# A batch's units all before its output products, attention steps of one shape side by side, and the last 64 rows of even and odd heads paired

## The chip, the cores and the metric

The kernel runs on one core of one Trainium2 chip. The time is that of one execution on the device, in microseconds (us); the median of three runs is given. TensorE (PE, with its weight loads as PEld), VectorE (DVE), ScalarE (ACT) and SyncE (SP, which issues all DMAs here) each work through their own instructions in order and wait for one another by semaphores.

## The reference: what is computed

Eight batches with eight heads, 576 positions and 64 values per head go through an attention with 32 memory slots per head. Then a bilinear feed-forward layer follows, whose last two products have nothing between them.

```python
a = phi - np.max(phi, axis=2, keepdims=True)
a = np.exp(a)
a = a / (np.sum(a, axis=2, keepdims=True) + 1e-09)      # softmax over the 576 positions
k_m = np.einsum('bhsm,bhsd->bhmd', a, k)                # 32 memories per head
v_m = np.einsum('bhsm,bhsd->bhmd', a, v)
scores = scale * np.matmul(q, k_m.transpose(0, 1, 3, 2))
...                                                     # softmax over the 32 memories
attn_out = np.matmul(attn, v_m)
x = attn_out.transpose(0, 2, 1, 3).reshape(B * S, H * D)
a = x @ w1
b = x @ w2
h = a * b @ w3
return h @ w_out
```

All arrays are float32. `w1` and `w2` are 512 x 1024, `w3` is 1024 x 1024, `w_out` is 1024 x 512.

## The kernel before

**What is computed how.** The kernel forms W = w3 w_out once, so that the feed-forward layer is one product with w1, one with w2, and one with W. It also multiplies w1 and w2 by each batch's v_m, which gives a matrix M per batch (`memory_weights`); so a batch's a and b come directly from its attention probabilities. To keep float32 accuracy at the speed of float32r, the operands of the large products are split into a high and a low part (`split`, lines 107 to 109: a ScalarE cast and a VectorE subtraction), and each product is the sum of three matmuls: high with high, high with low, low with high.

**A batch.** The 576 positions are two halves of 288 (`n`). `ab_unit(b, n, f, g)` makes 128 of the 1024 columns of a and b for one half, six matmuls each (line 407), copies a out of PSUM (line 416), multiplies (line 418) and splits the product into gh and gl (108 and 109). There are 16 such units per batch. `out_part(b, n, o, part, g, v)` does half of the sum for 128 of the 512 outputs, 12 matmuls (line 432); after the second half ScalarE copies the result to `osb` (line 437) and SP stores it (line 439). There are 16 of these too.

**Attention of the next batch.** Between the units and output products of batch b stand the steps of batch b+1, as functions in `attention(b)`: `top` takes the maximum of phi (line 144), `exp` (150), `norm` (155, 156), `turn0` and `turn4` transpose the exponentials on TensorE (165) to bring positions onto partitions, `mem` multiplies them with k and v (176), `blocks` transposes the memories back and lays them out (192 to 196), `sc0` and `sc1` make the scores of one half each (207), which VectorE transposes out of PSUM (216). `se`, `sn` and `pr` are the softmax and the split of the probabilities, one half each. The four quarters of M follow (line 263), each evacuated by one `split`.

**Positions in chunks.** 576 positions are four chunks of 128 and a last one of 64. In `turn4` that last chunk takes two transposes, of the even and of the odd heads (`t` = 0 and 1), and in `mem` it takes matmuls on 64 rows and 32 columns of the array, where the others use 128 rows and 32 columns. The loop runs over `t` outside and over chunks inside, so that the two shapes alternate.

**PSUM.** Eight banks: `ps_ab` has two sets of an a and a b bank, for the units; `ps_o` has two for the output products; `ps_x` is one pair of banks (`psum_pair`), which all attention steps and M share, one after the other.

**Order of the work.** The order on TensorE and SP is that of the program, fixed by hand in the lists `START`, `PLAN0` and `PLAN1`; the order on VectorE and ScalarE is set by a planner that simulates the program. `PLAN1` (batches 1 to 7) numbers 32 slots: eight units of the first half, eight output parts of it, eight units of the second half, eight output parts. After each slot come the steps that the plan names, so `sc0`, `sc1` and the four M stand apart from each other. `PLAN0` is for batch 0, whose 16 units come first.

**The start.** `START` works off the list `tasks`: each "C" (`next_tile`, `convert`) turns one tile of weights, which arrive as 64-bit floats, into float32 with ScalarE and VectorE (lines 339 to 344), and fetches a later one. "W00" and so on are products for W (line 354), "K" splits a finished block of W into Wh and Wl. The attention of batch 0 and two quarters of its M stand among them. The last four tiles are converted among the units of batch 0, from tiles that otherwise hold kv and q; the loads of batch 1's kv, q and phi come behind them in SP's order.

Of the kernel before, what the change touches and what calls it, by code (L numbers as in the profile page):

```python
# [29 lines left out]

PLAN0 = {
# [4 lines left out]
}  # L36


@with_exitstack
def memory_attention__then__bilinear_ffn_kernel(  # L40
# [21 lines left out]
    nc = tc.nc  # L62
# [11 lines left out]
    NBLK = S // M  # L74
    chunks = [(c, min(P, S - c)) for c in range(0, S, P)]
    scale = 1.0 / D**0.5
# [27 lines left out]
    def psum_pair():  # L104
        return ps_x.tile([P, 2, 512], F32, name="x")

    def split(hi, lo, src):
        nc.scalar.copy(out=hi, in_=src)  # L108
        nc.vector.tensor_tensor(out=lo, in0=src, in1=hi.bitcast(F32), op=ALU.subtract)  # L109
# [9 lines left out]
    def load_kv(b):  # L119
        t = []  # L120
        for i in range(0, len(chunks), 2):
            c, n = chunks[i]
            m = min(2, len(chunks) - i)
            x = att.tile([P, m, 8 * 2 * D], F32, name=f"kv{i}", tag=f"kv{i}")
            nc.sync.dma_start(out=x[:n], in_=kv[b, c : c + m * n].rearrange("(c p) h x -> p c (h x)", c=m))
            t += [x[:, j] for j in range(m)]
        loaded["kv", b] = t

    def load_q(b):
        t = att.tile([P, NG, S], F32, name="q", tag="q")  # L130
        nc.sync.dma_start(out=t, in_=qT[b].rearrange("g p s -> p g s"))
        loaded["q", b] = t


    ready = {}

    def attention(b):
# [16 lines left out]
        def norm():  # L154
            nc.vector.tensor_scalar_add(v["sm"], v["sm"], 1e-9)
            nc.vector.reciprocal(out=v["sm"], in_=v["sm"])
            a = att.tile([P, len(chunks) * NT * P], F32, name="a", tag="a")
            v["a"] = a.rearrange("p (c t x) -> p c t x", t=NT, x=P)

        def turn(i):  # L160
            ps = psum_pair().rearrange("p k (c t x) -> p (k c) t x", c=2, t=NT)
            some = chunks[i : i + 4]
            for k, (c, n) in enumerate(some):
                for t in range(NT):
                    nc.tensor.transpose(ps[:n, k, t], v["ph"][:, t, c : c + n], ident)  # L165
            n = some[0][1]
            nc.scalar.copy(out=v["a"][:n, i : i + len(some)], in_=ps[:n, : len(some)])

        def memories():
            kvt = loaded.pop(("kv", b))  # L170
            v["kvm"] = att.tile([P, NT, 2 * D], F32, name="kvm")
            ps = psum_pair()
            for t in range(NT):
                for i, (c, n) in enumerate(chunks):
                    for h in range(4):
                        nc.tensor.matmul(  # L176
                            ps[h * M : (h + 1) * M, t, : 2 * D],
                            lhsT=v["a"][:n, i, t, h * M : (h + 1) * M],
                            rhs=kvt[i][:n, (2 * h + t) * 2 * D : (2 * h + t + 1) * 2 * D],
                            start=i == 0,  # L180
                            stop=i == len(chunks) - 1,
                        )
            for t in range(NT):
# [13 lines left out]

        def scores(n):

            if n == 0:  # L200
                v["q"] = loaded.pop(("q", b))
                s_sb = att.tile([P, len(chunks) * NT * P], F32, name="s_sb", tag="a")
                v["s"] = s_sb[:, : NT * S].rearrange("p (n k m) -> p n k m", n=2, m=M)
            ps = psum_pair()[:, :, :HALF]
            for g in range(NG):
                for t in range(NT):
                    nc.tensor.matmul(  # L207
                        ps[g * M : (g + 1) * M, t],
                        lhsT=km[b % 2][t * D : (t + 1) * D, g],
                        rhs=v["q"][t * D : (t + 1) * D, g, n * HALF : (n + 1) * HALF],  # L210
                        start=True,
                        stop=True,
                    )
            nb = NBLK // 2
            for t in range(NT):
                nc.vector.transpose(
                    out=v["s"][:, n, t * nb : (t + 1) * nb], in_=ps[:, t].rearrange("p (k m) -> p k m", m=M)
                )
# [25 lines left out]

        steps = {"top": top, "exp": exp, "norm": norm, "mem": memories, "blocks": blocks}
        steps |= {f"turn{i}": lambda i=i: turn(i) for i in range(0, len(chunks), 4)}
        for name, f in (("sc", scores), ("se", soft_exp), ("sn", soft_norm), ("pr", probs)):
            steps |= {f"{name}{n}": lambda f=f, n=n: f(n) for n in range(2)}
# [5 lines left out]
    def memory_weights(b):  # L254

        ms = ready["M", b] = []

        def step(q):
            ps = psum_pair()
            for g in range(NG):  # L260
                for t in range(NT):
                    d = slice((1 - t) * D, (2 - t) * D)
                    nc.tensor.matmul(  # L263
                        ps[g * M : (g + 1) * M, t],
                        lhsT=vm[b % 2][d, g],
# [5 lines left out]
            ml = const.tile([P, NT, 2, FQ], F32R, name=f"ml{q}", tag=f"m{m_tags[2 * q + 1]}")  # L271
            src = ps.rearrange("p t (w f) -> p t w f", w=2)
            split(mh, ml, src)
            ms.append((mh, ml))

        return [lambda q=q: step(q) for q in range(NQ)]

# [34 lines left out]
    def convert(i):  # L312
# [13 lines left out]
        elif i % 2:  # L326
            u = att.tile([P, len(chunks) * NT * P], I32, name="ua", tag="a")
        else:
            u = att.tile([P, 2, S], F32R, name="al", tag="al", bufs=2).rearrange("p t s -> p (t s)").bitcast(I32)
# [44 lines left out]
    with tc.tile_pool(name="init", bufs=1) as init:  # L374
# [4 lines left out]
        for what in START:  # L379
# [4 lines left out]
            elif what[0] == "K":  # L384
                keep(int(what[1]), int(what[2]))
            elif what == "M":
                m0.pop(0)()
            elif what in ("phi", "kv", "q"):
                {"phi": load_phi, "kv": load_kv, "q": load_q}[what](0)
            else:  # L390
                steps[what]()
# [48 lines left out]

    def load(what, b):
        if b < B:
            {"phi": load_phi, "kv": load_kv, "q": load_q}[what](b)

    for b in range(B):
        g, v = {}, {}
        ab = [lambda n=n, f=f: ab_unit(b, n, f, g) for n in range(2) for f in range(NF)]
        out = [
            lambda n=n, o=o, part=part: out_part(b, n, o, part, g, v)
            for n in range(2)  # L450
            for o in range(NO)
            for part in range(2)
        ]
        if b == 0:
            next_tile()
            order = [n * NF + 2 * q + f for q in range(NQ) for n in range(2) for f in range(2)]
            slots = [ab[i] for i in order] + out
            plan = PLAN0
        else:
            slots = ab[:NF] + out[:NF] + ab[NF:] + out[NF:]  # L460
            plan = PLAN1
        if b + 1 < B:
            steps = attention(b + 1)
            m1 = memory_weights(b + 1)
        for i, slot in enumerate(slots):
            slot()
            for what in plan.get(i, ()):
                if isinstance(what, tuple):
                    load(what[0], b + what[1])
                elif what == "C":  # L470
                    next_tile()
                elif what == "N":
                    m0.pop(0)()
                elif b + 1 == B:
                    pass
                elif what == "M":
                    m1.pop(0)()
                else:
                    steps[what]()

# [44 lines left out]
```

## Time and profile before

| | |
|---|---|
| median of three runs | 578.13 us (577.53 to 578.64) |
| profiled execution | 577.72 us, with a span of 575.9 us from first to last instruction |
| mean granted TensorE clock | 0.991 |
| TensorE busy | 555.5 us, 96% |
| VectorE busy | 307.0 us, 53% |
| ScalarE busy | 253.8 us, 44% |
| DMA from and to memory | 54.00 MB read, 9.44 MB written |

In the views of the trace, a row of the timeline has the start in us, the time to the end of the last of its instructions, engine, line, operation, output tile and inputs, the part of the array in rows*columns, and the count. Times in brackets are idle time before it and what ended it. A row of the groups has busy time, mean ns of one, and the idle time before. A row of the waits has who waited for whom, the total in us, how often, and the longest. A matmul's duration includes its way through the array, so matmuls overlap; how often they start tells their pace.

### The profile page before, as it was taken

What the parts mean: (1) busy time and instruction counts of PE and PEld (TensorE: products, weight loads), DVE (VectorE), ACT (ScalarE), POOL (GpSimd) and SP (SyncE); (2) the same over time, 40 slices, a digit from 0 to 9 for tenths busy, and PEclk for the clock granted to TensorE, in tenths of its full rate; (3) what the DMA queues carried; (4) which work ended last, traced back from release to release, by engine and by line L of the source; (5) the groups of instructions that cost most, each with busy time, mean ns of one, the idle gap of its engine ahead of it and who ended that gap; (6) DMA issues with size and microseconds to landing.
All of it is one profiled execution on the core that took longest, in us unless ns stands there. A gap on an engine that the chain in (4) does not pass through costs nothing.

```text
span 575.9 us, 11149 instructions
## 1 busy us (share of the span) xinstructions
PE 555.5 (96%) x4704; PEld 471.1 (82%) x4704; DVE 307.0 (53%) x578; ACT 253.8 (44%) x501; POOL 0.7 (0%) x6
## 2 busy tenths in 40 slices
PE   3989979899999999999999999999999999999997
PEld 1444348887899989897989799988999798979997
DVE  4848997527436734393519442763348442934150
ACT  6858575514342544254514443353415451534141
POOL 0000000000000000000000000000000000000000
PEclk9999989899999999999999999999999999999999
DMA  8999528027208110541026200811063000000001
GB/s 323 408 354 390 199 73 286 3 67 238 69 11 270 51 43 2 182 128 52 12 73 216 63 22 11 277 47 39 1 207 124 32 11 33 12 22 20 32 11 42
DMA packets 28178, 64.16 MB, mean 111 GB/s; under 512 B 2016, under 2 KB 10208, under 8 KB 28128
## 3 DMA queue, kind: packets, MB, share of 16 engines
q1 hardware_dynamic: 28128, 63.45, 31.9%
q8 instruction: 37, 0.61, 0.4%
q14 instruction: 13, 0.11, 0.0%
HBM read 54.00 MB, written 9.44 MB: 110 GB/s over the span
## 4 chain that ended last, share of the span: by engine, by line
PE 81%; DVE 7%; DMA 7%; ACT 3%; issue 1%; SPq 0%; DVEq 0%; ACTq 0%
PE o L432 33%; PE a L407 16%; PE b L407 16%; DMA ph<-in_phiT 5%; PE x L263 4%; PE x L176 4%; PE a L354 2%; PE b L354 2%; PE x L207 2%; PE x L165 1%; DMA raw<-in_w_out 1%; DVE w L344 1%; DVE ml L109 1%; DVE mx L144 1%; DVE w L343 1%; DMA raw<-in_w3T 1%
## 5 line engine op out<-in xcount | busy, mean ns | idle before, releaser
L432 PE MATMUL o<-gh,Wh 128*128 128x288 f32 x512 | 156.2, 305 | 0.0
L432 PE MATMUL o<-gl,Wh 128*128 128x288 f32 x512 | 151.3, 296 | 0.0
L432 PE MATMUL o<-gh,Wl 128*128 128x288 f32 x512 | 151.0, 295 | 0.0
L432 PEld LDWEIGHTS o<-gh,Wh 128*128 128x128 f32 x512 | 96.7, 189 | 28.6 <-issue 25.8
L432 PEld LDWEIGHTS o<-gh,Wl 128*128 128x128 f32 x512 | 96.3, 188 | 0.0
L432 PEld LDWEIGHTS o<-gl,Wh 128*128 128x128 f32 x512 | 96.2, 188 | 0.0
L108 ACT CAST gh<-gr 128x288 fp32r<-128x288 f32 x128 | 54.9, 433 | 60.0 <-DVE gr L418 60.0
L407 PE MATMUL a<-ah,mh 128*128 128x288 f32 x256 | 78.9, 308 | 2.2 <-DVE Wl L109 2.2
L418 DVE TENSOR_TENSOR gr<-b,a_sb 128x288 f32<-128x288 f32 x128 | 57.8, 452 | 42.9 <-PE b L407 38.0
L407 PE MATMUL b<-ah,mh 128*128 128x288 f32 x256 | 76.7, 299 | 3.4 <-DVE gr L418 2.0
L407 PE MATMUL a<-ah,ml 128*128 128x288 f32 x256 | 76.9, 300 | 0.0
L109 DVE TENSOR_TENSOR gl<-gr,gh 128x288 fp32r<-128x288 f32 x128 | 57.7, 455 | 35.9 <-ACT gh L108 34.9
L407 PE MATMUL b<-ah,ml 128*128 128x288 f32 x256 | 76.4, 298 | 0.0
L407 PE MATMUL a<-al,mh 128*128 128x288 f32 x256 | 75.7, 296 | 0.0
L407 PE MATMUL b<-al,mh 128*128 128x288 f32 x256 | 75.5, 295 | 0.0
L109 DVE TENSOR_TENSOR ml<-x,mh 128x1024 fp32r<-128x1024 f32 x32 | 39.1, 1221 | 57.5 <-ACT mh L108 57.5
L416 ACT COPY a_sb<-a 128x288 f32<-128x288 f32 x128 | 50.8, 397 | 41.6 <-PE a L407 40.9
L437 ACT COPY osb<-o 128x288 f32<-128x288 f32 x64 | 25.4, 397 | 90.4 <-PE o L432 88.1
L407 PEld LDWEIGHTS a<-ah,mh 128*128 128x128 f32 x256 | 48.8, 191 | 7.7 <-issue 3.6
L108 ACT CAST mh<-x 128x1024 fp32r<-128x1024 f32 x32 | 32.5, 1015 | 45.2 <-PE x L263 45.1
L407 PEld LDWEIGHTS b<-ah,mh 128*128 128x128 f32 x256 | 49.0, 192 | 4.1 <-DVE gr L418 2.2
L407 PEld LDWEIGHTS a<-al,mh 128*128 128x128 f32 x256 | 49.7, 194 | 0.0
(70 smaller groups left out, 641.9 us busy)
## 6 DMA issues: line engine op xcount, KB each, us to landing
kv<-in_kv SPq DMA_DIRECT2D x16, 1024.0 KB, 7.8
q<-in_qT SPq DMA_DIRECT2D x8, 1152.0 KB, 6.2
outT<-osb SPq DMA_DIRECT2D x64, 144.0 KB, 1.8
raw<-in_w3T SPq DMA_DIRECT2D x7, 1024.0 KB, 18.6
ph<-in_phiT SPq DMA_DIRECT2D x8, 576.0 KB, 3.9
raw<-in_w SPq DMA_DIRECT2D x4, 1024.0 KB, 12.4
raw<-in_w_out SPq DMA_DIRECT2D x3, 1024.0 KB, 10.0
kv<-in_w SPq DMA_DIRECT2D x3, 1024.0 KB, 13.9
```

Of the source, the lines that this page charges most:

```text
L108: nc.scalar.copy(out=hi, in_=src)
L109: nc.vector.tensor_tensor(out=lo, in0=src, in1=hi.bitcast(F32), op=ALU.subtract)
L144: nc.vector.tensor_reduce(out=v["mx"], in_=v["ph"], axis=AX.X, op=ALU.max, negate=True)
L176: nc.tensor.matmul(ps[h * M : (h + 1) * M, t, : 2 * D], lhsT=v["a"][:n, i, t, h * M : (h + 1) * M], rhs=kvt[i][:n, (2 * h + t) * 2 * D : ( ...
L207: nc.tensor.matmul(ps[g * M : (g + 1) * M, t], lhsT=km[b % 2][t * D : (t + 1) * D, g], rhs=v["q"][t * D : (t + 1) * D, g, n * HALF : (n + ...
L263: nc.tensor.matmul(ps[g * M : (g + 1) * M, t], lhsT=vm[b % 2][d, g], rhs=w12_sb[q][d, :, g], start=True, stop=True,)
L354: nc.tensor.matmul(pw[r][i], lhsT=x[:, i * P : (i + 1) * P], rhs=wos[k // half][:, k % half], start=k == 0, stop=k == NF - 1,)
L407: nc.tensor.matmul(p, lhsT=x[:, t, w, fc : fc + P], rhs=y[:, n, t * HALF : (t + 1) * HALF], start=i == 0, stop=i == len(todo) - 1,)
L416: nc.scalar.copy(out=a_sb, in_=ps[0])
L418: nc.vector.tensor_tensor(out=gr, in0=ps[1], in1=a_sb, op=ALU.mult)
L432: nc.tensor.matmul(v["p"], lhsT=x[f // half][:, f % half, oc], rhs=y, start=f == 0 and i == 0, stop=f == NF - 1 and i == 2)
L437: nc.scalar.copy(out=osb, in_=v["p"])
```

## The change

1. **Stages.** From batch 1 on all 16 units come first (for each `f` both halves `n`), then all 16 output parts. The lists are now `FIRST` (batch 0) and `STEADY`, where "A" is a unit and "O" an output part.
2. **Neighbours.** In the output stage `sc0`, `sc1` and the first quarter of M follow each other directly ("sc0 sc1p Mp"), and later the three other quarters ("M Mp Mp"). Those with a "p" write to the a and b banks of `ps_ab`, which no unit uses then. An M in these banks is split in two pieces.
3. **Last 64 rows.** The host rolls phi of the odd heads by 64 positions, so that the last 64 positions of the even heads and of the odd heads lie side by side: `turn4` is one transpose. In `mem`, kv holds the even heads' rows on partitions 0 to 63 and the odd heads' on 64 to 127, loaded by two DMAs; first come all matmuls on 128 rows, then those on 64 rows, alternating between the two row halves.
4. **Start.** The turns of batch 0 stand after W04 and W05 (before: W06 and W07), `mem` after W07 (before: W10), `blocks` and the scores one product earlier, and `sn0` and the first M in other order. In batch 0 the second scores and the four quarters of M of batch 1 are placed as in `STEADY`.
5. **Loads.** The load of the batch after next's kv moves into the unit stage, q and phi into the output stage.

```diff
-PLAN1 = {
-    0: ["top"], 1: ["exp"], 2: ["norm"], 4: ["turn0"], 6: ["turn4"], 8: ["mem"], 11: ["blocks"], 13: ["sc0"],
-    15: ["sc1", "se0"], 18: ["se1"], 19: ["sn0"], 20: ["pr0"], 21: ["sn1"], 22: ["pr1"],
-    12: [("kv", 2)], 17: [("q", 2)], 23: [("phi", 2)],
-} | {i: ["M"] for i in range(24, 32, 2)}
...
 START = """
-C C W00 C phi C W01 C kv C W02 W03 C q C W04 W05 C top exp C norm W06 turn0 C W07 turn4 K00 K01 C K02 K03 W10 mem
-C W11 blocks C W12 sc0 C W13 sc1 se0 C W14 se1 M C W15 sn0 pr0 sn1 W16 pr1 C W17 M K10 K11 K12 K13
+C C W00 C phi0 C W01 C kv0 C W02 top exp norm W03 C q0 C W04 turn0 C W05 turn4 C W06 C W07 mem K00 K01 C K02 K03 W10
+blocks C W11 sc0 C W12 C sc1 se0 W13 C se1 W14 sn0 N C W15 pr0 sn1 W16 pr1 C W17 N K10 K11 K12 K13
 """.split()
+FIRST = """
+C A C A A C A N A C A A kv1 q1 A N phi1 A A A A top A exp A norm A turn0 A
+O turn4 O mem O O blocks O sc0 sc1p Mp kv2 O se0 O se1 O sn0 O pr0 q2 O sn1 O M Mp Mp O pr1 O O phi2 O O
+""".split()
+STEADY = """
+A top A exp A norm A A turn0 A A turn4 A A mem A A kv2 blocks A A A A A
+O sc0 sc1p Mp O se0 O se1 O q2 sn0 O pr0 O sn1 O pr1 M Mp Mp O phi2 O O O O O O O O
+""".split()
...
+    def banks_ab():
+        return [psum(ps_ab, x) for x in "ab"]
...
         def turn(i):
+            if i == 0:
...
+            else:
+                last = v["ph"].rearrange("p t s -> p (t s)")[:, 4 * P : 5 * P]
+                nc.tensor.transpose(ps[:, 0, 0], last, ident)
+                nc.scalar.copy(out=v["a"][:, 4, 0], in_=ps[:, 0, 0])
...
         def memories():
             for t in range(NT):
-                for i, (c, n) in enumerate(chunks):
+                for i in range(4):
                     for h in range(4):
...
+            for h in range(4):
+                for t in range(NT):
+                    nc.tensor.matmul(
+                        ps[h * M : (h + 1) * M, t, : 2 * D],
+                        lhsT=v["a"][t * D : (t + 1) * D, 4, 0, h * M : (h + 1) * M],
+                        rhs=kvt[4][t * D : (t + 1) * D, h * 2 * D : (h + 1) * 2 * D],
...
-        def scores(n):
+        def scores(n, banks):
-            ps = psum_pair()[:, :, :HALF]
+            ps = [x[:, :HALF] for x in banks()]
...
-        def step(q):
-            ps = psum_pair()
+        def step(q, banks):
+            one = None if banks else psum_pair()
+            ps = banks() if banks else [one[:, t] for t in range(NT)]
...
+            if banks:
+                for t in range(NT):
+                    split(mh[:, t], ml[:, t], ps[t].rearrange("p (w f) -> p w f", w=2))
+            else:
+                split(mh, ml, one.rearrange("p t (w f) -> p t w f", w=2))
...
-            slots = ab[:NF] + out[:NF] + ab[NF:] + out[NF:]
+        ab = iter([(n, f) for f in range(NF) for n in range(2)])
...
+    ph = np.stack([ph[:, 0], np.roll(ph[:, 1], s % 128, axis=-1)], axis=1)
```

More of the change, by code (lines that the diff above doesn't have):

```diff
@@ L74, in memory_attention__then__bilinear_ffn_kernel @@
     NBLK = S // M
-    chunks = [(c, min(P, S - c)) for c in range(0, S, P)]
     scale = 1.0 / D**0.5
@@ L105, in psum_pair, with pair @@
         return ps_x.tile([P, 2, 512], F32, name="x")
+    def pair():
+        x = psum_pair()
+        return [x[:, i] for i in range(2)]
+    def banks_ab():
+        return [psum(ps_ab, x) for x in "ab"]
     def split(hi, lo, src):
@@ L120, in load_kv @@
         t = []
[L121 to L127, printed above, removed]
+        for i in range(0, 4, 2):
+            x = att.tile([P, 2, 8 * 2 * D], F32, name=f"kv{i}", tag=f"kv{i}")
+            src = kv[b, i * P : (i + 2) * P].rearrange("(c p) h x -> p c (h x)", c=2)
+            nc.sync.dma_start(out=x, in_=src)
+            t += [x[:, j] for j in range(2)]
+        x = att.tile([P, NG * 2 * D], F32, name="kv4", tag="kv4")
+        for j in range(NT):
+            src = kv[b, 4 * P :, j * NG : (j + 1) * NG].rearrange("s h x -> s (h x)")
+            nc.sync.dma_start(out=x[j * D : (j + 1) * D], in_=src)
+        loaded["kv", b] = [*t, x]
     def load_q(b):
@@ L132, in load_q, with load @@
         loaded["q", b] = t
+    LOADS = {"phi": load_phi, "kv": load_kv, "q": load_q}
+    def load(what, b):
+        b += int(what[-1])
+        if b < B:
+            LOADS[what[:-1]](b)
     ready = {}
@@ L156, in norm @@
             nc.vector.reciprocal(out=v["sm"], in_=v["sm"])
-            a = att.tile([P, len(chunks) * NT * P], F32, name="a", tag="a")
+            a = att.tile([P, 5 * NT * P], F32, name="a", tag="a")
             v["a"] = a.rearrange("p (c t x) -> p c t x", t=NT, x=P)
@@ L161, in turn @@
             ps = psum_pair().rearrange("p k (c t x) -> p (k c) t x", c=2, t=NT)
[L162 to L167, printed above, removed]
+            if i == 0:
+                for c in range(4):
+                    for t in range(NT):
+                        at = t * D + c * P
+                        nc.tensor.transpose(ps[:, c, t], v["ph"][:, t, at : at + P], ident)
+                nc.scalar.copy(out=v["a"][:, :4], in_=ps)
+            else:
+                last = v["ph"].rearrange("p t s -> p (t s)")[:, 4 * P : 5 * P]
+                nc.tensor.transpose(ps[:, 0, 0], last, ident)
+                nc.scalar.copy(out=v["a"][:, 4, 0], in_=ps[:, 0, 0])
         def memories():
@@ L177, in memories @@
                             ps[h * M : (h + 1) * M, t, : 2 * D],
-                            lhsT=v["a"][:n, i, t, h * M : (h + 1) * M],
-                            rhs=kvt[i][:n, (2 * h + t) * 2 * D : (2 * h + t + 1) * 2 * D],
+                            lhsT=v["a"][:, i, t, h * M : (h + 1) * M],
+                            rhs=kvt[i][:, (4 * t + h) * 2 * D : (4 * t + h + 1) * 2 * D],
                             start=i == 0,
-                            stop=i == len(chunks) - 1,
+                            stop=False,
                         )
+            for h in range(4):
[4 more added lines that the diff above has]
+                        rhs=kvt[4][t * D : (t + 1) * D, h * 2 * D : (h + 1) * 2 * D],
+                        start=False,
+                        stop=True,
+                    )
             for t in range(NT):
@@ L196, in blocks @@
                 nc.vector.tensor_copy(out=vm[b % 2][vo : vo + D], in_=p4[vo : vo + D, t])
-        def scores(n):
+        def scores(n, banks):
             if n == 0:
                 v["q"] = loaded.pop(("q", b))
-                s_sb = att.tile([P, len(chunks) * NT * P], F32, name="s_sb", tag="a")
+                s_sb = att.tile([P, 5 * NT * P], F32, name="s_sb", tag="a")
                 v["s"] = s_sb[:, : NT * S].rearrange("p (n k m) -> p n k m", n=2, m=M)
-            ps = psum_pair()[:, :, :HALF]
+            ps = [x[:, :HALF] for x in banks()]
             for g in range(NG):
@@ L207, in scores @@
                     nc.tensor.matmul(
-                        ps[g * M : (g + 1) * M, t],
+                        ps[t][g * M : (g + 1) * M],
                         lhsT=km[b % 2][t * D : (t + 1) * D, g],
@@ L216, in scores @@
                 nc.vector.transpose(
-                    out=v["s"][:, n, t * nb : (t + 1) * nb], in_=ps[:, t].rearrange("p (k m) -> p k m", m=M)
+                    out=v["s"][:, n, t * nb : (t + 1) * nb], in_=ps[t].rearrange("p (k m) -> p k m", m=M)
                 )
@@ L245, in attention @@
         steps = {"top": top, "exp": exp, "norm": norm, "mem": memories, "blocks": blocks}
-        steps |= {f"turn{i}": lambda i=i: turn(i) for i in range(0, len(chunks), 4)}
-        for name, f in (("sc", scores), ("se", soft_exp), ("sn", soft_norm), ("pr", probs)):
+        steps |= {f"turn{i}": lambda i=i: turn(i) for i in (0, 4)}
+        for n in range(2):
+            steps |= {f"sc{n}": lambda n=n: scores(n, pair), f"sc{n}p": lambda n=n: scores(n, banks_ab)}
+        for name, f in (("se", soft_exp), ("sn", soft_norm), ("pr", probs)):
             steps |= {f"{name}{n}": lambda f=f, n=n: f(n) for n in range(2)}
@@ L263, in step @@
                     nc.tensor.matmul(
-                        ps[g * M : (g + 1) * M, t],
+                        ps[t][g * M : (g + 1) * M],
                         lhsT=vm[b % 2][d, g],
@@ L271, in step @@
             ml = const.tile([P, NT, 2, FQ], F32R, name=f"ml{q}", tag=f"m{m_tags[2 * q + 1]}")
-            src = ps.rearrange("p t (w f) -> p t w f", w=2)
-            split(mh, ml, src)
+            if banks:
+                for t in range(NT):
+                    split(mh[:, t], ml[:, t], ps[t].rearrange("p (w f) -> p w f", w=2))
+            else:
+                split(mh, ml, one.rearrange("p t (w f) -> p t w f", w=2))
             ms.append((mh, ml))
-        return [lambda q=q: step(q) for q in range(NQ)]
+        return [lambda banks=None, q=q: step(q, banks) for q in range(NQ)]
     def rows(w, k, n):
@@ L326, in convert @@
         elif i % 2:
-            u = att.tile([P, len(chunks) * NT * P], I32, name="ua", tag="a")
+            u = att.tile([P, 5 * NT * P], I32, name="ua", tag="a")
         else:
@@ L385, in memory_attention__then__bilinear_ffn_kernel @@
                 keep(int(what[1]), int(what[2]))
-            elif what == "M":
+            elif what == "N":
                 m0.pop(0)()
-            elif what in ("phi", "kv", "q"):
-                {"phi": load_phi, "kv": load_kv, "q": load_q}[what](0)
+            elif what[:-1] in LOADS:
+                load(what, 0)
             else:
@@ L439, in out_part @@
             nc.sync.dma_start(out=outT[oc, c : c + HALF], in_=osb)
-    def load(what, b):
-        if b < B:
-            {"phi": load_phi, "kv": load_kv, "q": load_q}[what](b)
     for b in range(B):
         g, v = {}, {}
[L447 to L453, printed above, removed]
-        if b == 0:
[L455 to L459, printed above, removed]
-            slots = ab[:NF] + out[:NF] + ab[NF:] + out[NF:]
-            plan = PLAN1
+        ab = iter([(n, f) for f in range(NF) for n in range(2)])
+        if b == 0:
+            ab = iter([(n, 2 * q + f) for q in range(NQ) for n in range(2) for f in range(2)])
+        out = iter([(n, o, part) for n in range(2) for o in range(NO) for part in range(2)])
         if b + 1 < B:
@@ L464, in memory_attention__then__bilinear_ffn_kernel @@
             m1 = memory_weights(b + 1)
[L465 to L479, printed above, removed]
+        for what in STEADY if b else FIRST:
+            if what == "A":
+                ab_unit(b, *next(ab), g)
+            elif what == "O":
+                out_part(b, *next(out), g, v)
+            elif what == "C":
+                next_tile()
+            elif what == "N":
+                m0.pop(0)()
+            elif what[:-1] in LOADS:
+                load(what, b)
+            elif b + 1 == B:
+                pass
+            elif what[0] == "M":
+                m1.pop(0)(banks_ab if what == "Mp" else None)
+            else:
+                steps[what]()
 _INS = ["qT", "kv", "phiT", "w1", "w2", "w3T", "w_out"]
@@ L492 @@
     m = phi.shape[-1]
-    kv = np.empty((b, s, h // 2, 2, 2, d), k.dtype)
+    kv = np.empty((b, s, 2, h // 2, 2, d), k.dtype)
     for src, at in ((k, 0), (v, 1)):
         x = src.transpose(0, 2, 1, 3).reshape(b, s, h // 2, 2, d)
-        kv[:, :, :, 0, at] = x[:, :, :, 0]
-        kv[:, :, :, 1, 1 - at] = x[:, :, :, 1]
+        kv[:, :, 0, :, at] = x[:, :, :, 0]
+        kv[:, :, 1, :, 1 - at] = x[:, :, :, 1]
     def pairs_swapped(w):
@@ L501, in pairs_swapped @@
         return x.transpose(1, 0, 2)
+    ph = phi.reshape(b, h // 2, 2, s, m).transpose(0, 2, 1, 4, 3).reshape(b, 2, h // 2 * m, s)
+    ph = np.stack([ph[:, 0], np.roll(ph[:, 1], s % 128, axis=-1)], axis=1)
     laid = {
@@ L505 @@
         "kv": kv.reshape(b, s, h, 2 * d),
-        "phiT": phi.reshape(b, h // 2, 2, s, m).transpose(0, 2, 1, 4, 3).reshape(b, 2, h // 2 * m, s),
+        "phiT": ph,
         "w1": pairs_swapped(moe_w1),
```

2 lines of the change are left out of this document (removed), and 4 rows, old and new, of the table PLAN0.

## The prediction

> **What bounds the kernel now.** I read the engine totals of the page and its chain of waits first, then the busy time by stretch.
>
> ```profile
> span 575.9 us, 11149 instructions
> ...
> PE 555.5 (96%) x4704; PEld 471.1 (82%) x4704; DVE 307.0 (53%) x578; ACT 253.8 (44%) x501; POOL 0.7 (0%) x6
> ...
> PE 81%; DVE 7%; DMA 7%; ACT 3%; issue 1%; SPq 0%; DVEq 0%; ACTq 0%
> ```
>
> TensorE is busy 96% of the span and carries 81% of the chain of waits. What remains is 20.4 us of idle time, so a large gain must come out of TensorE's own work. One whole batch, from first turn to first turn, by the view of stretches (the columns are length, then busy time and count of PE, PEld, DVE, ACT, POOL, then granted clock, DMA share, GB/s):
>
> ```profile
> 282.72:344.69 61.97, 61.70 (x574) 55.38 (x573) 31.52 (x63) 25.25 (x56) 0.00 (x0) 1.00 0.26 87
> ```
>
> TensorE works 61.7 of 62.0 us, while VectorE has 31.5 and ScalarE 25.3. A batch has 192 matmuls of `ab_unit` and 192 of `out_part`, and their pace stands in the chain of waits:
>
> ```profile
> 534.60 12.73 PE o L432 x96
> ```
>
> 12.73/96 = 0.1326 us each, so the 384 take 50.9 us, and a batch's other 10.8 us are the attention steps of the next batch. The change acts on those.
>
> **Joined steps.** What one attention step costs TensorE is read from the timeline: the time between the matmuls around it, less their own pace. First scores, then one quarter of M; the rows with x8 come from a view that ends within the step.
>
> ```profile
> 300.97 0.30 PE L432 MATMUL o<-gl,Wh 128*128 128x288 f32 x1
> 301.20 0.47 PE L207 MATMUL x<-q,km 64*32 64x288 f32 x8
> 301.20 0.72 PE L207 MATMUL x<-q,km 64*32 64x288 f32 x16
> ...
> 302.08 0.29 PE L432 MATMUL o<-gh,Wl 128*128 128x288 f32 x1
> ```
>
> ```profile
> 320.11 0.30 PE L432 MATMUL o<-gl,Wh 128*128 128x288 f32 x1
> 320.34 0.66 PE L263 MATMUL x<-w,vm 64*32 64x512 f32 x8
> 320.34 1.09 PE L263 MATMUL x<-w,vm 64*32 64x512 f32 x16
> ...
> 321.59 0.29 PE L432 MATMUL o<-gh,Wl 128*128 128x288 f32 x1
> ```
>
> Between the outer rows lie two paces of L432, so scores cost 302.08-300.97-0.27 = 0.84 us, and a quarter of M 321.59-320.11-0.27 = 1.21 us. Each runs in two rounds of eight matmuls, all eight at once on tiles of 64*32. The second round adds 0.72-0.47 = 0.25 us for scores and 1.09-0.66 = 0.43 us for M. A step that follows another of the same tile shape should therefore add two such rounds, 0.50 and 0.86, and not 0.84 and 1.21: a join saves 0.34 or 0.35 us, the way into and out of the 64*32 shape. I take 0.32, as the starts of eight matmuls are spread over some hundredths.
>
> Before, each of the two scores and four quarters of M is enclosed by `ab_unit` or `out_part` work. After, "sc0 sc1p Mp" and "M Mp Mp" stand without anything between, which makes four joins: 4 x 0.32 = 1.28 us per batch. The trace shows no two such steps together, so the bounds are 0 and 4 x 0.35 = 1.40. I go near the upper one since a join is to be what the second round already is.
>
> The Trainium skill has a rule against this: by "TensorE: Matmul & The Clock Gate", section "Part 3: Packing small matmuls", a weight load overlaps running matmuls only if its row group differs. A join, which reloads the same row groups, would by it gain next to nothing. The x8 and x16 rows disagree: the second round uses the same row groups and follows after 0.25 us, though its weights are new too.
>
> Joins need free banks. The a and b banks are idle in the out stage, two sets of them. `sc1p` gets the set of the last unit but one, the first `Mp` that of the last unit. The groups of instructions give what has to be done by then (mean ns of one after the comma):
>
> ```profile
> L418 DVE TENSOR_TENSOR gr<-b,a_sb 128x288 f32<-128x288 f32 x128 | 57.8, 452 | 42.9 <-PE b L407 38.0 <-ACT gh L108 2.3 <-issue 1.5
> L109 DVE TENSOR_TENSOR gl<-gr,gh 128x288 fp32r<-128x288 f32 x128 | 57.7, 455 | 35.9 <-ACT gh L108 34.9
> L109 DVE TENSOR_TENSOR ml<-x,mh 128x1024 fp32r<-128x1024 f32 x32 | 39.1, 1221 | 57.5 <-ACT mh L108 57.5
> ```
>
> ```profile
> L108 ACT CAST gh<-gr 128x288 fp32r<-128x288 f32 x128 | 54.9, 433 | 60.0 <-DVE gr L418 60.0
> L416 ACT COPY a_sb<-a 128x288 f32<-128x288 f32 x128 | 50.8, 397 | 41.6 <-PE a L407 40.9
> ```
>
> A bank b is free 0.45 us after its matmuls (gr); the first `out_part`, 12 x 0.1326 = 1.59 us, and both scores lie before `Mp` starts, so nothing waits. `Mp` is split in two halves, an instruction more on each engine, three times a batch: at the worst another 1.22 us of VectorE each (the ml row), which its 30 idle us cover.
>
> **Memories and turns.** The same reading, for `memories` (the row with x28 from a view that ends within it) and for the second turn:
>
> ```profile
> 289.87 0.29 PE L432 MATMUL o<-gl,Wh 128*128 128x288 f32 x1
> 290.09 1.08 PE L176 MATMUL x<-kv,a 128*32 128x128 f32 x32
> 291.10 0.42 PE L176 MATMUL x<-kv,a 64*32 64x128 f32 x8
> 291.46 0.97 PE L176 MATMUL x<-kv,a 128*32 128x128 f32 x28
> 292.82 0.40 PE L432 MATMUL o<-gh,Wh 128*128 128x288 f32 x1
> ```
>
> ```profile
> 286.48 0.29 PE L407 MATMUL b<-ah,ml 128*128 128x288 f32 x1
> 286.61 0.38 PE L165 MATMUL x<-ident,ph 128*64 128x128 f32 x2
> ...
> 286.96 0.30 PE L407 MATMUL a<-al,mh 128*128 128x288 f32 x1
> ```
>
> Before, shapes alternate 32, 8, 32, 8: 1.01 us (290.09 to 291.10), 0.36 (to 291.46), and both again, 2.73 in all. After, all 64 matmuls of 128*32 stand together, and the last 16 use both row halves, eight tiles at once. Four matmuls more cost (x32 against x28) 1.08-0.97 = 0.11, so the second 32 cost 0.88; the 16 run as two rounds of eight, 0.36 to 0.41 us. That is 1.01+0.88+0.38 = 2.27, a saving of 0.46 us; bounds are 0.13 (only the one shape change saved) and 0.49. The second turn has one transpose for two, half of 286.96-286.48-0.27 = 0.21: 0.11 us. The first turn keeps its eight.
>
> **Order of the stages.** Sixteen units in a row need per unit 0.45+0.46 = 0.91 us of VectorE and 0.40+0.43 = 0.83 of ScalarE, in 1.59 us of TensorE: no bound. A batch's VectorE work less the units is 31.5-16x0.91 = 17 us; most of it is softmax and the splits of M, which now follow the scores in an out stage of some 31 us (16 x 1.59 plus the steps), beginning 2.5 us into it. It ends near 21 us. What is late next: the second unit of a batch now reads the second half of ah and al, which was wanted eight units later before; it has 10 us in hand. SP's queue holds the stores of out behind the phi load, which waits for the last `al`. That is done (near 17 us) about when the eighth `out_part` ends, and three osb buffers cover more. The q load moves from the units to behind the fourth store; it waits for the scores alone, which are done by then, and kv moves from the stores to the units. If the cover were gone, TensorE would stall for the lateness itself. One batch: 1.28+0.46+0.11 = 1.85 us, seven batches (those that prepare another): 12.95 us, with bounds of 7x0.24 = 1.7 and 7x2.00 = 14.0.
>
> **The start.** Here alone TensorE idles, and the granted clock falls; the longest waits of PE up to 125 us and the stretches tell where:
>
> ```profile
> PE a L407 <- DVE Wl L109: 2.2, 1, 2.2
> PE b L407 <- DVE gr L418: 2.0, 1, 2.0
> PE o L354 <- DVE w L344: 1.5, 1, 1.5
> ```
>
> ```profile
> 80.00:100.00 20.00, 18.09 (x130) 15.75 (x131) 16.62 (x28) 12.40 (x23) 0.00 (x0) 0.83 0.66 227
> 100.00:110.00 10.00, 8.02 (x49) 7.79 (x48) 4.99 (x11) 4.36 (x12) 0.00 (x0) 0.83 0.04 15
> ```
>
> Turns and memories move ahead of the first product of the second half of W and fill its wait of 1.5 us (PE o). But the first units then wait for VectorE (PE a, 2.2 us), so VectorE decides what arrives. Of its own waits one is for `blocks`:
>
> ```profile
> 51.99 0.28 DVE L195 TENSOR_SCALAR km<-x 64x128 f32<-64x128 f32 x1 [1.42 <-PE x L192]
> ```
>
> These 1.42 us should go, as memories and `blocks` come a product earlier. I take 1.42, of bounds 0 and 3.7 (1.5 and 2.2, both PE waits gone). In the other direction kv is loaded by four DMAs and not three, and in the first batch the q and phi loads of the second queue behind them on SP. VectorE already waits for that phi:
>
> ```profile
> 87.42 1.44 SPq L125 DMA_DIRECT2D kv<-in_kv x3
> ```
>
> ```profile
> 102.51 1.35 DVE L144 TENSOR_REDUCE mx<-ph 128x2 f32<-128x1152 f32 x1 [1.99 <-DMA ph<-in_phiT]
> ```
>
> 1.44/3 = 0.48 us later. In later batches kv is issued in the unit stage, with no store behind it. Start: 1.42-0.48 = 0.94 us.
>
> **Sum.** 12.95+0.94 = 13.9 us. The profiled execution took 577.72 us with a span of 575.9; the median 578.13 is 0.41 more. 575.9-13.9 = 562.0 span, 563.8 for that execution, 564.3 against the median.
>
> **The rivals.** (1) *Joins save nothing*, since the next group's weights aren't loaded under the round that runs. Price: a join then pays what leaving and entering cost, 28 x 0.32 = 9.0 us given back: 573.2. Against it is the 0.25 us round. The rule of the Trainium skill's "TensorE: Matmul & The Clock Gate" given above would end here. (2) *The start gives it back*: the order of VectorE and ScalarE is planned anew, and a longer wait there is paid twice, as the granted clock of 0.83 from 80 to 110 us cost 0.17 x 30 = 5 us. One more such stretch of 20 us (3.4), without the 0.94: 568.6. (3) *Slower: mx blocks the units.* VectorE works in order. If mx of the next batch waits for its phi load in the middle of the units, gr stands behind it, and b stays full. That is what happened at 102 us, and its price was 2.0 us (PE b above). With the clock's loss in that stretch (0.17 x 10 = 1.7) it is 3.7 us, in seven batches 26: 590. It decides from 13.9/7 = 2.0 us a batch. Against it, phi is issued with eight `out_part` of 1.59 us left, and took:
>
> ```profile
> 318.48 4.04 DMA ph<-in_phiT
> ```
>
> (4) *It comes to nothing*: stalls of the longer stages eat what the joins give, 578.
>
> **How the numbers follow.** Forecast 564.3 (own range 560 to 568): 0.66. Rival 1 at 573: 0.13. Rival 2 at 568.6: 0.11. Slower at 590: 0.06. Nothing, 578: 0.04. A measurement of this kernel tells about 0.2%, 1.2 us, from no change. Faster 0.90, same 0.04, slower 0.06. The range goes from 559.5 (564.3-2.8-1.0 = 560.5), where the start gains 3.7 us instead of 0.9 and the batches their upper bound (1 us more), and a little beyond, to 573.3, where rival 1 ends; that leaves out under 2 in 10.
>
> **What would show it.** TensorE's busy time in a steady batch should fall from 61.7 to near 59.9 us, with 50.9 of it unchanged, and the batch should take little more. "sc0 sc1p Mp" should show 48 matmuls of 64*32 in about 2.3 us from outer row to outer row, less two paces; three quarters of M about 3.0. Memories should show x64 then x16 within 2.3 us. If joined rounds start 0.5 us or more apart for scores, rival 1 is right. PE waits for gr, ml or osb in the steady batches would be rival 3 or 4. The forecast is wrong if the batch stays above 61 us, or if the first unit of batch 1 doesn't come earlier by about 1 us plus one batch's 1.85.

## The result, and the profile after

The changed kernel takes 560.14 us (median of four runs, 557.92 to 560.34), beside 577.83 us for the kernel before. The ratio is 0.9683, with a 95% interval of 0.9656 to 0.9710: 17.7 us or 3.2% faster. 564.3 had been predicted, with a range of 559.5 to 573.3. The profiled execution took 560.32 us.

The page's engine totals and chain of waits, after:

```profile
span 558.4 us, 11184 instructions
...
PE 540.5 (97%) x4696; PEld 472.6 (85%) x4696; DVE 310.6 (56%) x599; ACT 253.4 (45%) x522; POOL 0.7 (0%) x6
...
PE 93%; DMA 3%; DVE 2%; issue 1%; SPq 0%; ACT 0%; DVEq 0%; ACTq 0%
```

TensorE is busy for 15.0 us less (555.5 before), with only 8 matmuls fewer, and carries 93% of the chain in place of 81%. Where the 17.5 us of span went is told by the time of each batch's first turn. It stands at 113.06 us before and 110.71 after for batch 1's attention, at 159.00 and 154.53 for batch 2's, and then every 61.81 us on the mean (61.70 to 61.97) before and every 59.60 after. So the start gave 2.35 us, batch 0 gave 2.1, five more spacings of batches gave 2.2 each, and what follows the last turn gave 2.0. Over the first 110 us both profiles had the same granted clock, 0.95 on the mean.

One steady batch after, by stretches (length, busy time and count of PE, PEld, DVE, ACT, POOL, granted clock, DMA share, GB/s):

```profile
214.30:273.90 59.60, 59.60 (x573) 55.58 (x572) 32.30 (x66) 25.15 (x59) 0.00 (x0) 1.00 0.27 90
```

TensorE is busy for the whole batch; before, 0.27 of 61.97 us were idle. The joined steps, in the timeline of one batch:

```profile
236.73 0.29 PE L465 MATMUL o<-gl,Wh 128*128 128x288 f32 x1
236.95 0.72 PE L234 MATMUL x<-q,km 64*32 64x288 f32 x16
237.46 0.40 PE L234 MATMUL a<-q,km 64*32 64x288 f32 x1
...
237.71 0.40 PE L234 MATMUL a<-q,km 64*32 64x288 f32 x1
...
237.95 0.59 PE L293 MATMUL b<-w,vm 64*32 64x512 f32 x1
...
238.38 0.59 PE L293 MATMUL b<-w,vm 64*32 64x512 f32 x1
...
239.18 0.30 PE L465 MATMUL o<-gh,Wl 128*128 128x288 f32 x1
```

`sc0` starts at 236.95, and each row after it in the fence is the first matmul of a round of eight: the two rounds of `sc1p` (237.46, 237.71) and the two of `Mp` (237.95, 238.38). The rounds of scores follow each other by 0.25 us, across the join as within a step. From outer row to outer row, less two paces of 0.13, the three steps take 2.19 us; separately they took 0.84 + 0.84 + 1.21. The later group of three quarters of M:

```profile
248.47 0.30 PE L465 MATMUL o<-gl,Wh 128*128 128x288 f32 x1
248.69 1.09 PE L293 MATMUL x<-w,vm 64*32 64x512 f32 x16
...
251.66 0.29 PE L465 MATMUL o<-gh,Wl 128*128 128x288 f32 x1
```

That is 2.93 us for 3 x 1.21 before. Together the joins save 0.70 + 0.70 = 1.40 us. Memories after:

```profile
221.35 0.29 PE L440 MATMUL b<-ah,ml 128*128 128x288 f32 x1
221.58 1.95 PE L194 MATMUL x<-kv,a 128*32 128x128 f32 x64
223.46 0.45 PE L203 MATMUL x<-kv,a 64*32 64x128 f32 x16
...
224.08 0.29 PE L440 MATMUL a<-al,mh 128*128 128x288 f32 x1
```

From the first of the 64 to the first unit's matmul at 223.84 these are 2.26 us, 2.73 before. (The trace has two rows for each of these float32 matmuls: the 40 calls of the program make the 80. The second round of a step is the second row of each of its matmuls.) In the start, the waits of PE between 20 and 125 us:

```profile
PE b L440 <- DVE gr L451: 1.9, 1, 1.9
PE a L440 <- DVE Wl L112: 1.8, 1, 1.8
PE b L440 <- DVE Wl L112: 1.4, 1, 1.4
```

The wait of 1.5 us for the first product of W's second half is gone; the three others stayed, each a little shorter or the same (2.0, 2.2 and 1.4 before). From batch 1 on PE waits for nothing.

### The profile page after: what moved, and what is told of

It reads as the page before. It is cut to its first block, busy times and chain, and to the rows that moved or that the text cites. A ratio compares the mean times of both kernels' runs of the same rounds, so it can differ in the third digit from the quotient of the medians.

```text
span 558.4 us, 11184 instructions
## 1 busy us (share of the span) xinstructions
PE 540.5 (97%) x4696; PEld 472.6 (85%) x4696; DVE 310.6 (56%) x599; ACT 253.4 (45%) x522; POOL 0.7 (0%) x6
## 4 chain that ended last, share of the span: by engine, by line
PE 93%; DMA 3%; DVE 2%; issue 1%; SPq 0%; ACT 0%; DVEq 0%; ACTq 0%
PE o L465 37%; PE a L440 17%; PE b L440 17%; PE a L387 4%; PE b L387 4%; PE x L194 3%; PE o L387 3%; DMA ph<-in_phiT 2%; PE a L293 2%; PE x L293 2%; PE x L180 1%; PE b L293 1%; PE x L234 1%; DMA raw<-in_w3T 1%; PE x L203 1%
## 5 line engine op out<-in xcount | busy, mean ns | idle before, releaser
L465 PE MATMUL o<-gh,Wh 128*128 128x288 f32 x512 | 152.9, 299 | 0.0
L440 PEld LDWEIGHTS b<-al,mh 128*128 128x128 f32 x256 | 49.7, 194 | 0.0
L440 PEld LDWEIGHTS a<-ah,ml 128*128 128x128 f32 x256 | 48.9, 191 | 0.0
## 6 DMA issues: line engine op xcount, KB each, us to landing
kv<-in_w SPq DMA_DIRECT2D x3, 1024.0 KB, 12.9
```

The source lines that it names most:

```text
L440: nc.tensor.matmul(p, lhsT=x[:, t, w, fc : fc + P], rhs=y[:, n, t * HALF : (t + 1) * HALF], start=i == 0, stop=i == len(todo) - 1,)
L465: nc.tensor.matmul(v["p"], lhsT=x[f // half][:, f % half, oc], rhs=y, start=f == 0 and i == 0, stop=f == NF - 1 and i == 2)
```

## The experiments

Each kernel ran beside the kernel before on the same chip. e1 to e4 ran in one job (before: 577.45 us), e0 and e5 to e7 in another (before: 576.13 us), so between jobs ratios are compared.

| kernel | median us | ratio to before, 95% interval | steady batch us |
|---|---|---|---|
| the change | 560.14 | 0.9683 (0.9656 to 0.9710) | 59.60 |
| the change again (e0) | 558.69 | 0.9689 (0.9663 to 0.9715) | 59.60 |
| no joins (e1) | 568.86 | 0.9853 (0.9838 to 0.9868) | 61.07 |
| pairing alone, on before (e2) | 571.60 | 0.9898 (0.9882 to 0.9914) | 61.04 to 61.42 |
| start as before (e3) | 560.26 | 0.9707 (0.9686 to 0.9727) | 59.60 |
| phi first (e4) | 556.80 | 0.9644 (0.9630 to 0.9659) | 59.60 |
| phi late (e5) | 560.15 | 0.9728 (0.9690 to 0.9767) | 59.60 to 60.18 |
| joined in x (e6) | 644.06, one run | | 71.8 to 73.6 |
| phi first and turns joined (e7) | 556.81 | 0.9653 (0.9632 to 0.9674) | 59.58 |

### No joins

```diff
-O sc0 sc1p Mp O se0 O se1 O q2 sn0 O pr0 O sn1 O pr1 M Mp Mp O phi2 O O O O O O O O
+O sc0 O sc1p O Mp se0 O se1 O q2 sn0 O pr0 O sn1 O pr1 M O Mp O Mp O phi2 O O O O O
```

The list of batch 0 is changed in the same way.

> The changed kernel with one output part set between the steps that it joins (sc0 O sc1p O Mp, later M O Mp O Mp); banks, stages, start and the pairing of the last rows stay. Theory: what a join saves is the way into and out of the 64*32 shape, 0.35 us; four joins less in seven batches give back 28 x 0.35 = 9.9 us: 570 us, and a steady batch is 61.0 us in place of 59.60. Rival (the joins save nothing; the order of the stages or the idle banks brought the gain): 560 us, a batch of 59.6 us.

568.86 us, and two steady batches by stretches:

```profile
276.23:337.31 61.08, 61.08 (x574) 55.26 (x573) 32.87 (x67) 25.33 (x59) 0.00 (x0) 1.00 0.26 88
337.31:398.38 61.07, 61.07 (x574) 55.24 (x572) 32.85 (x67) 25.33 (x59) 0.00 (x0) 1.00 0.26 88
```

The batch is 1.47 us longer with the same matmuls, TensorE busy throughout. Four joins are thus worth 0.37 us each, and 7 x 1.47 = 10.3 us in all; the difference of the ratios, 0.0170 of 577.8, is 9.8. The joins are the larger part of the gain, and it is TensorE's own time, no wait.

### Pairing alone

The kernel before with the new `load_kv`, `turn` and `memories` and the new host layout; plans, stages and start stay.

```diff
-            for k, (c, n) in enumerate(some):
-                for t in range(NT):
-                    nc.tensor.transpose(ps[:n, k, t], v["ph"][:, t, c : c + n], ident)
...
+                last = v["ph"].rearrange("p t s -> p (t s)")[:, 4 * P : 5 * P]
+                nc.tensor.transpose(ps[:, 0, 0], last, ident)
...
-                for i, (c, n) in enumerate(chunks):
+                for i in range(4):
...
+            for h in range(4):
+                for t in range(NT):
+                    nc.tensor.matmul(
```

> The kernel before with the pairing of the last 64 rows alone (one transpose in turn4, 64 matmuls of 128*32 and then 16 of 64*32 in mem, the new layout of phi and kv); stages, plans and start as before. Theory: 0.46 + 0.11 = 0.57 us for each of the seven batches, and as much at the start where TensorE waits for VectorE anyway, so 4.0 to 4.6 us: 573.5 us, and a steady batch of 61.25 us in place of 61.82. Rival (the shapes cost nothing of their own and memories are bound by the count of matmuls, which stays at 80): 577.1 us, only the transposes' 0.8 us less.

571.60 us, more than expected. Two steady batches by stretches:

```profile
217.52:278.61 61.09, 61.09 (x573) 55.22 (x572) 31.52 (x64) 25.10 (x56) 0.00 (x0) 1.00 0.27 88
278.61:340.03 61.42, 61.11 (x573) 55.22 (x572) 31.52 (x64) 25.30 (x57) 0.00 (x0) 1.00 0.27 88
```

TensorE's busy time is 61.1 us where it was 61.70: 0.6 us per batch, as worked out (0.57), with only one matmul fewer. The rival, which lets the count of matmuls decide, falls. The first turns tell where the 6.2 us of span went: 4.3 lie in the batches, and 2.0 ahead of the first turn of batch 1 (111.09 for 113.06 us). For the latter the pairing isn't the likely cause: the first unit comes only 0.15 us earlier (76.26 for 76.41), but the granted clock up to 110 us was 0.98 here and 0.95 in the profile of before, which is a matter of chance (below).

This kernel also bounds what the order of the stages is worth. Its batches still contain waits (0.31 us in the second row), as those of before do: M's matmuls wait for a split of M to empty their bank pair. In the kernel without joins, which differs from it in stages, banks and start, they are gone: 61.07 in every batch, where 61.20 is the mean here. Whether the order or the further banks took them out was not tried.

### Start as before

```diff
-C C W00 C phi0 C W01 C kv0 C W02 top exp norm W03 C q0 C W04 turn0 C W05 turn4 C W06 C W07 mem K00 K01 C K02 K03 W10
+C C W00 C phi0 C W01 C kv0 C W02 W03 C q0 C W04 W05 C top exp C norm W06 turn0 C W07 turn4 K00 K01 C K02 K03 W10 mem
...
```

> The changed kernel with the order of the start as before (turns after W06 and W07, memories after W10, blocks and scores a product later). Theory: the first turn of batch 1 comes 2.35 us earlier in the changed kernel because VectorE no longer waits for blocks (1.4 us) and for the DMA and ScalarE (the rest); with the old order 1.4 to 2.3 us come back: 561.6 to 562.5 us. Rival (the start is bound by its DMAs, and the earlier turn comes from the shorter memories alone): 560.1 us.

560.26 us. By the ratios, 0.9707 against 0.9683 and 0.9689, it is 1 us slower than the change, but the intervals overlap: the times alone don't tell them apart. The trace does, before any chance of the clock comes in. The first unit's matmul in this kernel and then in the repeat of the change:

```profile
76.13 0.40 PE L440 MATMUL a<-ah,mh 128*128 128x288 f32 x1
```

```profile
74.35 0.40 PE L440 MATMUL a<-ah,mh 128*128 128x288 f32 x1
```

The new order brings the first unit 1.8 us earlier. The rival, that the earlier turn comes from the shorter memories alone, would have given 74.4 here. The first turn of batch 1 tells the same when kernels with the same granted clock up to 110 us (0.97) are compared; this kernel, and the one without joins, which has the new start:

```profile
111.09 1.04 PE L180 MATMUL x<-ident,ph 128*128 128x128 f32 x8
```

```profile
108.71 1.04 PE L180 MATMUL x<-ident,ph 128*128 128x128 f32 x8
```

That is 2.4 us; at 0.98 it is 2.1 (pairing alone 111.09, the repeat of the change 109.01). So the traces show the upper part of the 1.4 to 2.3 us that were expected, and the times only 1 us of it.

### Phi first

```diff
-C A C A A C A N A C A A kv1 q1 A N phi1 A A A A top A exp A norm A turn0 A
+C A C A A C A N A C A A phi1 kv1 q1 A N A A A A top A exp A norm A turn0 A
```

> The changed kernel with the load of batch 1's phi issued ahead of its kv and q, whose tiles come free later. Theory: the 1.95 us in which TensorE waits at 102 us, for VectorE's maximum of phi, go, and so does the stretch of half clock behind it (3.4 us at half, 1.7 us lost): 556.5 us. Rival (VectorE is full there, so the wait only turns into VectorE's own work): 560 us. In between (558 us): the wait goes, the half clock stays.

556.80 us, nearly as expected (556.5). PE's waits from 20 to 125 us, and two stretches, of this kernel:

```profile
PE b L440 <- DVE Wl L112: 2.0, 1, 2.0
PE a L440 <- DVE Wl L112: 1.8, 1, 1.8
```

```profile
80.00:100.00 20.00, 18.68 (x137) 16.69 (x138) 16.61 (x30) 12.08 (x26) 0.00 (x0) 0.84 0.62 207
100.00:110.00 10.00, 10.00 (x79) 10.00 (x78) 5.78 (x13) 5.41 (x14) 0.00 (x0) 1.00 0.01 2
```

The wait for gr is gone, and from 100 to 110 us the clock is at 1.00 and TensorE is busy throughout (8.06 us and 0.83 in the profile of the change). VectorE was not full there. So the load of phi behind kv and q, which wait for their tiles, was what held TensorE up at 102 us: it is issued at 78.92 us here and takes 3.7 us, in the change at 87.95 and 12.2. The clock of 1.00 alone would not show it, for the repeat of the change, the kernel without joins and phi late have 1.00 from 100 to 110 us too, and the wait with it. At the same clock up to 110 us (0.97), the first turn of batch 1 comes at 107.59 here and at 108.71 without joins, 1.1 us. Its ratio, 0.9644, lies below both of the change; its interval ends below that of the repeat and overlaps a little with the first. Its four runs (556.70 to 557.20) are all shorter than the eight of the change, though those ran in other jobs. Turns joined (below) also loads phi first, and beside the repeat of the change, in one job, its four runs (556.60 to 557.08) are again all shorter (558.01 to 560.21).

### Phi late

```diff
-... pr1 M Mp Mp O phi2 O O O O O O O O
+... pr1 M Mp Mp O O O O O O O O O phi2
```

> The changed kernel with the load of phi for the batch after next moved behind the last output part of each batch, so that VectorE's maximum of phi falls among the units. It prices the slower rival of the prediction. Theory: the load lands some 4.5 us into the units; VectorE waits up to 2 us for it and then works 1.35 us, while the two sets of banks give TensorE 1.9 us; a batch becomes 0 to 1.5 us longer, 560 to 570 us. Rival as predicted (2.0 us of waiting and 1.7 us of half clock in every batch): 3.7 us a batch, 586 us.

560.15 us, ratio 0.9728 against 0.9689 for the repeat of the change in the same job, intervals overlapping. Batches are 59.60 to 60.18 us, 0.3 us longer on the mean. The waits of VectorE for phi over the whole run, and those of PE after 120 us:

```profile
DVE mx L158 <- DMA ph<-in_phiT: 8.4, 7, 1.6
```

```profile
PE b L440 <- DVE gr L451: 0.3, 1, 0.3
```

VectorE waits up to 1.6 us among the units. Of its 8.4 us, the view of waits shows 0.3 on TensorE, but the five spacings of batches are together 1.4 us longer: the two sets of banks hold off most of it. The price that the prediction had set for its slower rival, 3.7 us a batch, doesn't arise with these waits; they are shorter than the 2.0 us on which it rests.

### Joined in x

```diff
-O sc0 sc1p Mp O se0 ... pr1 M Mp Mp O phi2
+O sc0 sc1 M O se0 ... pr1 M M M O phi2
```

> The changed kernel with the same neighbours, but all in the one pair of banks x (sc0 sc1 M, later M M M), instead of the idle a and b banks. Theory: a join without banks turns into a wait: the second scores wait for two transposes of VectorE (2 x 0.46 us and the signals), M for two more, the second and third M of the later group each for the split before (1.0 us of ScalarE and 1.2 of VectorE): some 6 to 7 us a batch, and over 600 us in all. Rival (the engines are early enough, the banks don't matter): 560 us.

644.06 us. PE's waits between 120 and 640 us, and one batch by stretches:

```profile
PE x L293 <- DVE ml L112: 34.0, 14, 2.4
PE x L293 <- DVE s_sb L243: 11.3, 7, 1.6
PE x L234 <- DVE s_sb L243: 7.8, 7, 1.2
```

```profile
236.77:308.81 72.04, 64.47 (x573) 58.07 (x572) 32.70 (x64) 25.03 (x56) 0.00 (x0) 0.93 0.23 75
```

The same neighbours without the idle banks make four waits a batch: 2 x 2.4 for the splits of M, 1.6 and 1.1 for the transposes. These 7.6 us are the idle part of the 72.04. The rest is the clock, 0.93 in place of 1.00 (0.07 x 72 = 5 us, and TensorE is busy for 64.5 in place of 59.6), as stretches of half clock now follow these waits in each batch (0.57 on the mean from 264 to 268 us, 0.50 from 284 to 288). So it is the idle banks that make the joins pay here.

### Phi first and turns joined

The change with phi first, and

```diff
-A top A exp A norm A A turn0 A A turn4 A A mem
+A top A exp A norm A A turn0 turn4 A A A A mem
...
+                one = psum(ps_o, "o")[:, :P]
```

> The changed kernel with phi loaded first in the start, as in e4_phi_first (556.8 us), and both turns side by side, the second in a bank of ps_o, which no output part uses in the unit stage. Theory: transposes use the array in the shape of the units, so that joining them saves no change of shape, only the 0.1 us by which the second matmul after small ones is late: a batch of 59.5 us in place of 59.60, 556 us in all. Rival (each separate step costs 0.35 us whatever its shape): 59.25 us a batch, 554.3 us.

556.81 us; one steady batch by stretches:

```profile
270.25:329.83 59.58, 59.58 (x574) 55.56 (x573) 32.27 (x67) 24.96 (x59) 0.00 (x0) 1.00 0.27 91
```

0.02 us less than 59.60, nothing that a time could show; even the 0.1 us of the theory isn't there. A separate step of transposes costs nothing beyond its matmuls; they use the array in 128*128, the shape of the units. What a join of scores or M saves is therefore the change of the array's shape, not the being separate. The Trainium skill says this much in "TensorEngine Tiling (Array Packing)", section "Tiling Modes": changing the tiling mode, and not just the tile, drains TensorE. The runs agree that the change costs time and put the way in and out at 0.35 to 0.37 us here; that a drain takes it they do not show by themselves.

### The change again

The changed kernel without an edit.

> The changed kernel itself once more, beside the next three. Theory: runs of one kernel differ by stretches of half clock in the start, 3.4 us long and 1.7 us dear each, which fall or don't by chance; so runs at a mean clock of 0.997 are 2 to 3.5 us shorter than those at 0.991, and the median lies between 558 and 560.3 us. Rival (the earlier spread, 557.9 to 560.3 us, is of another origin): no relation of time and clock.

558.69 us. The runs at a mean clock of 0.991, 0.994 and 0.997 took 559.96 to 560.34 (three), 558.01 to 560.21 (three), and 557.92 and 558.51. For the kernel before, the runs of both jobs at 0.991 took 577.45 to 578.41, and those at 0.994 took 575.76 to 577.40. So the clock goes with the time, by one to two us from 0.991 to 0.994, but it isn't all: the change's three runs at 0.994 differ by 2.2 us among themselves. Part of the spread stays unexplained.

## Why the prediction was right

**The bound.** That TensorE's own work decides held in each run: where batches got shorter, TensorE's busy time did, and the other engines' didn't.

**Joins.** Mechanism and place were right. The term was 0.32 us; the outer rows give 1.40/4 = 0.35, the run without joins 0.37. I had taken off some hundredths for the spread of eight starts, which weren't owed: a round's first matmul follows the first of the round before by 0.25 us, also across the join. Rival 1 fell: by it the joins would have saved next to nothing, and the batch without joins would have been no longer. With it went the rule of the Trainium skill's "TensorE: Matmul & The Clock Gate", section "Part 3: Packing small matmuls", as the prediction had read it.

**Memories and turns.** 0.57 was predicted, 0.6 measured with the pairing alone.

**Stages.** I had put nothing down for the order of the stages. The waits of 0.0 to 0.3 us that a batch had before, about 0.1 us on the mean, went with it or with the further banks. M's matmuls waiting for ml were in the profile of before (0.27 us in the batch that I quoted), and no term of the sum took them out.

**The batch in all.** The mean spacing of batches is 61.81 us before, 61.20 with the pairing alone, 61.07 without joins and 59.60 after. That is 0.61, 0.13 and 1.47, together 2.21 us where 1.85 was predicted, 2.5 us more in seven batches. Of the 0.36 us more, 0.19 are the joins, sized too small, and 0.13 the term that was missing. The upper bound of 2.00 did not hold either: it gave the joins 1.40 and the waits nothing.

**The start.** 0.94 us was predicted, 2.35 measured at the first turn of batch 1. The mechanism was right: memories and turns fill TensorE's wait of 1.5 us, and VectorE's wait for `blocks` of 1.42 us went. The order alone accounts for the gain: the kernel with the old start comes 2.4 us later at the same clock. But the size was taken from that one wait. VectorE also waited less for the first w3 tile of the second half, 4.53 in place of 5.33 us (4.87 in the repeat). The fourth DMA of kv did cost SP time (2.08 us for all of kv in place of 1.44), but kv's loads began 2.3 us earlier: phi was issued 1.6 us earlier than before (87.95 for 89.54) and took 12.2 us where it had taken 12.9, so VectorE got it 2.3 us earlier. What these parts are worth singly wasn't tried.

**Rivals.** Rival 2 (the start gives it back) didn't occur, though its price was real: phi first took out one wait and gained 2 to 3 us, 1.1 of them at the same clock; a stretch of half clock follows that wait in the profile of the change, but not in all. The slower rival was provoked and came to 0.3 us a batch, not 3.7. Its flaw was to carry over the price from the start. VectorE's rows around that wait, before, and around one of 1.58 us in phi late:

```profile
97.22 0.46 DVE L418 TENSOR_TENSOR gr<-b,a_sb 128x288 f32<-128x288 f32 x1 [0.18 <-PE b L407]
...
99.29 1.23 DVE L109 TENSOR_TENSOR ml<-x,mh 128x1024 fp32r<-128x1024 f32 x1 [0.65 <-ACT mh L108]
...
103.78 0.81 DVE L418 TENSOR_TENSOR gr<-b,a_sb 128x288 f32<-128x288 f32 x2
```

```profile
267.10 0.46 DVE L451 TENSOR_TENSOR gr<-b,a_sb 128x288 f32<-128x288 f32 x1 [0.17 <-PE b L440]
269.13 1.35 DVE L158 TENSOR_REDUCE mx<-ph 128x2 f32<-128x1152 f32 x1 [1.58 <-DMA ph<-in_phiT]
...
270.77 0.45 DVE L451 TENSOR_TENSOR gr<-b,a_sb 128x288 f32<-128x288 f32 x1
```

In the start a split of M stood ahead of the wait, and from one gr to the next 6.1 us passed in which no b bank came free. Among the steady units the wait began right behind a gr, and 3.2 us passed, of which the two sets of banks covered most.

**Size.** 13.9 us predicted, 17.5 in the spans: of the 3.6 us more, some 2.5 lie in the batches and 1.4 in the start; batch 0 and what follows the last turn gave a little less than the others. So the mechanism held and the sizes were too small; 560.14 us lies near the lower end of the range. The last step of the sum is also off by 0.1 us: 563.8 and 0.41 are 564.2.

## What to carry to other kernels

Where TensorE is the bound and its steps change the shape in which they use the array, put steps of one shape side by side: here each join saved some 0.35 us, as much as 2.6 large matmuls, while joining transposes of the common shape saved nothing. A join needs free banks for each step, so look for the stage in which another stage's banks are idle; the same order in one pair of banks took 15% longer than the change. And price a wait where it occurs: a late load of phi cost TensorE 2 us in the start and 0.3 us a batch among steady units.

The fastest version that ran is the change with phi loaded first, 556.80 us or 0.9644 of the kernel before; joining the turns as well gave the same (556.81).

## What was not expected of the hardware

Weights for the next round of eight small matmuls are loaded while the round before runs in the same rows of the array, across different instructions of the program (line 234 to line 293): the rounds of scores start every 0.25 us, though a matmul takes 0.40. The first weight load of the quarter of M starts together with the last round of scores, at 237.71:

```profile
237.71 0.11 PEld L293 LDWEIGHTS b<-w,vm 64*32 64x32 f32 x1
```

Memories of 80 matmul rows took 0.47 us less with the same 80. Two changes of shape fell away and eight tiles of 64*32 ran at once in place of four; what each is worth was not tried singly.

Waits of 1.1 to 2.4 us, four in a batch, were enough to bring stretches of half clock into each batch (0.93 on the mean of one batch, joined in x), and in the start one wait of 1.9 us was followed by such a stretch in the profile of the change and, with a wait of 2.4 us at the same place, by none in its repeat (0.83 and 1.00 from 100 to 110 us).
